# Scaled copies of v in quarters and normalising products in halves on two engines, VectorE's reciprocal for the sums, and another set of ordering numbers in a fused attention and Mish kernel

## The chip, the core and the metric

The kernel runs on one core of a Trainium2 chip. The metric is the device time of one execution in microseconds (us), given as the median of several runs. Besides these, one execution is recorded by the hardware profiler; all rows below come from that one. TensorE multiplies matrices into PSUM, ScalarE evaluates functions (exponential and tanh here), VectorE and GpSimd do elementwise work, SyncE issues most of the DMAs. GpSimd does not read PSUM in this kernel.

## The reference

One input `x` of 2048 tokens by 640 goes through attention with 32 heads of 20 and through a dense layer with Mish; a sigmoid gate per token mixes the two.

```
qkv = (x @ wqkv)                       # 640 -> 3 x 32 heads x 20
scores = einsum("bhqd,bhkd->bhqk", q, k) * Dh ** -0.5
o = einsum("bhqk,bhkd->bhqd", softmax(scores), v)
a = o.reshape(B, S, D) @ wo
h = x @ w1 + b1                        # 640 -> 1536
b = (h * tanh(softplus(h))) @ w2       # Mish, 1536 -> 640
g = sigmoid((x * gate_w).sum(-1))
out = g * a + (1 - g) * b
```

## The kernel before

**Tiling.** Queries go in 4 chunks of 512, heads in 8 groups of 4 (20 rows of a head stand in 32 partitions, so the four heads of a group lie on the four row groups of TensorE). A *unit* is one head's scores for 128 keys by 512 queries: one PSUM bank. There are 2048 units, ordered by (chunk, head group); the last group's queries are cut into two halves of 256.

**A slot.** Three units form a slot; there are 683. `emit_s` puts the three score matmuls (line 1378) into one of two triples of PSUM banks, `emit_e` lets ScalarE take the exponential of the slot in one instruction (line 1400, into the ring `ETS`). In many slots (`choose`) the third unit is given to VectorE instead: ScalarE then takes two units, a *pair*, and `emit_x` evicts the third (line 1450) as a 16-bit integer that, read as a half-precision number, is a first approximation of the exponential. Up to four such units of one head group make a *batch*; `close` adds two shifted versions of the batch (lines 1486 to 1488), and `emit_off` multiplies all three by v on TensorE (line 1720), the third one by a *scaled copy* of v. Scores of slot s+2 need the banks that the exponential and the eviction of slot s have read.

**Scaled copies.** `VW` holds v times 199/256 for the head group in work. `scale` (lines 1674 to 1701) writes it when a group ends: 21 times as one VectorE instruction of 1344 columns, in the first groups as four quarters of 336 columns while v is still being made.

**Sums and normalising.** v has a column of ones, so row 0 of each head's product holds the softmax sums. At a group's end `group_done` copies the accumulated bank to `OUNG` (VectorE, line 1905), moves the four rows of sums through a DMA into `RR`, 128 partitions by 16 (line 1923, queue SP), and `invert` raises them to the power -1 on GpSimd (line 1927). A DMA writes them to `SUMS` in DRAM (line 1930), four more (`spread`, line 1936) read them back into `BCT`, each row repeated over 32 partitions, and `times` (line 1857) multiplies `OUNG` by `BCT`. The product goes to VectorE or, whole (`PARTS = 1`), to GpSimd. Its result is moved by four or five DMAs into the packed layout of the output projection (`move`, line 1850). All these DMAs stand in SyncE's one queue in the order of the program, with the projections' moves (lines 724, 751) and weight loads (lines 997, 1003, 1015).

**The Mish part.** `mish` runs per 1024 columns: tanh on ScalarE (line 1071), then scalars (line 1095) and four products (line 1104) on VectorE; a product may go in quarters to GpSimd.

**What sets the order.** The program is written by a planner (`Plan`, `attention`) that keeps a clock for each engine and adds costs from the table of constants at the top (`EXP`, `WIDE`, `SPREAD_TAIL`, ...). Jobs that are not tied to a slot wait in lists (`norm` for inverting and normalising, `scaled` for the copies, `blend` for Mish, `soon` for shifts); `work` lets VectorE take those that are ready before its next eviction, `settle` offers the head of a list to GpSimd if it fits behind VectorE's last instruction of kind "L" (one that reads and writes SBUF) and before VectorE's clock. `choose` compares VectorE's lead over ScalarE, corrected by `NUDGE[s // 8]`, with thresholds (`BEHIND`, `IDLE`), and decides which slots become pairs. A number in that table so moves rows everywhere behind it. On the chip each engine works its own list strictly in order and waits on semaphores.

## Time and profile before

| | |
|---|---|
| runs (us) | 753.31, 754.74, 753.92; median 753.92 |
| profiled execution (us) | 755.81, of it a span of 754.0 from the first to the last instruction |
| granted TensorE clock, mean | 0.998 |
| exponentials | 683: 492 pairs, 191 triples |
| VectorE evictions of score banks (line 1450) | 492 |
| first and last exponential start (us) | 9.39, 745.1 |

In the rows below PE is TensorE (PEld its weight loads), ACT ScalarE, DVE VectorE, POOL GpSimd, SPq SyncE's DMA queue. A row of the groups gives line, engine, operation, output and inputs with shapes, the count, then busy time in us and the mean duration of one in ns, then the engine's idle time in front of them in us and what ended it. A timeline row gives start and duration in us, and in brackets the idle time of the engine before it with what ended that. A row of the stretches gives the stretch, its length, and busy time and count for PE, PEld, DVE, ACT and POOL, the granted clock, the DMA share and GB/s.

### The profile page before, as it was taken

The numbers are of one execution on the slowest core, as the hardware profiler recorded it, in microseconds if no ns is written. First come the engines' busy times: TensorE is split into PE (matmuls) and PEld (weight loads), VectorE is DVE, ScalarE is ACT, GpSimd is POOL, SyncE is SP. The second block draws the span as 40 slices with busy tenths as digits, with TensorE's granted clock in tenths as the row PEclk, the third lists the DMA queues.
The fourth block names the chain that finished last, engine by engine and source line by source line (L and its number), as shares of the span: only waits on it lengthen the run. The fifth ranks groups of instructions, "written<-read, shape, count | busy, mean of one in ns | idle before, by whom it ended". The sixth has DMA issues, their size and how long they took to land.

```text
span 754.0 us, 19649 instructions
## 1 busy us (share of the span) xinstructions
PE 707.4 (94%) x8065; PEld 266.4 (35%) x8065; DVE 703.4 (93%) x1298; ACT 736.5 (98%) x715; POOL 188.6 (25%) x162
## 2 busy tenths in 40 slices
PE   8999999999998999999999999999999999999996
PEld 4334333333332343233333334333333333323232
DVE  4878898999898999989999999999999999999995
ACT  6999999999999999999999999999999999999996
POOL 8111101333212420212213322213204232223111
PEclk9999999999999999999999999999999999999999
DMA  8321321321233215112113302102222122011001
GB/s 188 105 63 42 99 70 35 101 67 53 65 107 101 70 47 163 39 42 56 54 44 108 95 21 73 60 21 76 82 55 71 55 60 80 20 33 31 18 18 47
DMA packets 81675, 49.62 MB, mean 66 GB/s; under 512 B 25474, under 2 KB 77562, under 8 KB 81578
## 3 DMA queue, kind: packets, MB, share of 16 engines
q1 hardware_dynamic: 80810, 48.16, 22.7%
q8 instruction: 67, 1.10, 0.6%
q14 instruction: 30, 0.25, 0.1%
q10 hardware_dynamic: 656, 0.10, 0.1%
q0 software_dynamic: 112, 0.01, 0.0%
HBM read 36.10 MB, written 7.52 MB: 58 GB/s over the span
## 4 chain that ended last, share of the span: by engine, by line
ACT 86%; PE 7%; DVE 3%; DMA 2%; POOL 0%; issue 0%; SPq 0%
ACT ETS L1400 83%; ACT REG L1071 2%; PE PS L1378 2%; PE PS L1720 2%; PE PS L575 2%; ACT W2R L1071 1%; DVE QT L1450 1%; DMA OTN<-in_A_x_dram 1%; DMA SUMS<-RR 1%; DMA BCT<-SUMS 1%; DVE KT L1450 0%; PE PS L785 0%; POOL RR L1927 0%; DMA RR<-OUNG 0%; PE PS L2152 0%
## 5 line engine op out<-in xcount | busy, mean ns | idle before, releaser
L1400 ACT ACTIVATE ETS<-PS 128x1024 bf16<-128x1024 f32 (+1 forms) x683 | 715.7, 1263 | 5.4 <-PE PS L1378 4.9
L1378 PE MATMUL PS<-QT,KT 32*128 32x512 bf16 (+1 forms) x2112 | 267.3, 378 | 34.0 <-ACT ETS L1400 23.7
L1927 POOL TENSOR_TENSOR RR<-RR,NEG 128x16 f32<-128x16 f32 x31 | 93.9, 3029 | 268.8 <-DMA RR<-OUNG 268.8
L1720 PE MATMUL PS<-ETS,V_all 128*21 128x512 bf16 (+1 forms) x1606 | 156.8, 375 | 0.0
L1378 PEld LDWEIGHTS PS<-QT,KT 32*128 32x128 bf16 x2112 | 67.7, 91 | 250.4 <-ACT ETS L1400 212.1
L1104 POOL TENSOR_TENSOR U<-U 128x256 f16<-128x256 f16 x77 | 50.9, 661 | 215.6 <-DVE U L1095 176.8
L1450 DVE TENSOR_SCALAR QT<-PS 128x512 int16<-128x512 f32 x123 | 82.4, 682 | 2.6 <-PE PS L1378 1.9
L575 PE MATMUL PS<-XB,REG 128*32 128x256 bf16 (+3 forms) x824 | 80.5, 294 | 2.0 <-DVE OUTT L1185 1.5
L1450 DVE TENSOR_SCALAR OTN<-PS 128x512 int16<-128x512 f32 x109 | 73.3, 681 | 2.3 <-PE PS L1378 2.0
L575 PE MATMUL PS<-W2R,HB 128*128 128x320 bf16 (+1 forms) x645 | 72.4, 300 | 0.2
L1450 DVE TENSOR_SCALAR PADS<-PS 128x512 int16<-128x512 f32 x101 | 67.9, 682 | 4.8 <-PE PS L1378 4.6
L575 PEld LDWEIGHTS PS<-XB,REG 128*32 128x32 bf16 (+1 forms) x824 | 39.5, 97 | 32.1 <-issue 21.1
L1720 PEld LDWEIGHTS PS<-ETS,V_all 128*21 128x21 bf16 x1606 | 39.1, 90 | 30.0 <-issue 25.5
L575 PEld LDWEIGHTS PS<-W2R,HB 128*128 128x128 bf16 (+1 forms) x645 | 33.1, 97 | 29.1 <-issue 14.7
L1450 DVE TENSOR_SCALAR KT<-PS 128x512 int16<-128x512 f32 x54 | 36.7, 684 | 4.0 <-PE PS L1378 3.7
L1104 DVE TENSOR_TENSOR U<-U 128x1024 f16<-128x1024 f16 (+3 forms) x71 | 38.6, 544 | 0.0
L1450 DVE TENSOR_SCALAR REG<-PS 128x512 int16<-128x512 f32 x56 | 38.0, 682 | 0.1
L1048 DVE TENSOR_TENSOR HB<-PS,B1T 128x512 bf16<-128x512 f32 x48 | 32.7, 681 | 0.4 <-PE PS L575 0.2
L1095 DVE TENSOR_SCALAR U<-U 128x1024 f16<-128x1024 f16 x72 | 30.1, 418 | 0.5
L1488 DVE TENSOR_SCALAR QT<-QT 128x2048 int16<-128x2048 int16 (+2 forms) x43 | 28.6, 667 | 0.7 <-PE PS L1720 0.7
L1104 POOL TENSOR_TENSOR HB<-U,HB 128x256 bf16<-128x256 f16 x28 | 18.7, 669 | 38.1 <-DVE U L1104 25.6
L1720 PE MATMUL PS<-QT,V_all 128*21 128x512 f16 x280 | 28.2, 388 | 0.0
(176 smaller groups left out, 801.8 us busy)
## 6 DMA issues: line engine op xcount, KB each, us to landing
REG<-in_B_w_dram SPq DMA_DIRECT2D x36, 320.0 KB, 3.2
BCT<-SUMS SPq DMA_DIRECT2D x124, 64.0 KB, 2.0
W2R<-in_B_w_dram SPq DMA_DIRECT2D x12, 320.0 KB, 3.4
KT<-KS SPq DMA_DIRECT2D x28, 128.0 KB
QT<-QS SPq DMA_DIRECT2D x112, 20.0 KB
QS<-WOQ SPq DMA_DIRECT2D x16, 128.0 KB, 1.7
KS<-OTN SPq DMA_DIRECT2D x16, 128.0 KB, 2.6
W2R<-in_B_w_dram SPq DMA_DIRECT2D x1, 1920.0 KB, 8.3
```

What stands on the lines that cost most here:

```text
L575: op = e.matmul(PS[at, bank, cols], w[:, at], x, start=start, stop=stop, **({"tile_position": (0, i * rows)} if parts > 1 else {}))
L1048: ev = dve(lambda e: e.tensor_tensor(hb, PS[:, bank, :].rearrange("p (i t) -> p i t", i=2), bias, ALU.add), [last, b_load, *b_read.get(hc ...
L1071: ex = pl.add("act", lambda e: e.activation(U, h, AF.Tanh, scale=0.5, bias=-MISH_AT), [ev, u_free[0]], cost=0.95)
L1095: return lambda e: e.tensor_scalar(dst, src, *ops)
L1104: return lambda e: e.tensor_tensor(dst[:, at], one[:, at], two[:, at], ALU.mult)
L1378: op = pl.add("pe", lambda e, i=i, g=real(g), tile=tile, j=j, cols=cols, c=c, of_q=of_q: e.matmul(scores(s)[:, i, cols], KT[32 * j:32 * j ...
L1400: e_op[s] = pl.add("act", lambda e: e.activation(EXPS[:, at:at + n, :], scores(s)[:, 0:n, :], AF.Exp, scale=SCALE, bias=LIFT if fast else ...
L1450: ev = dve_by(lambda e: e.tensor_scalar(block(batch["y"], n, I16), scores(s)[:, 2, :], SCALE * ULPS, BIAS, ALU.mult, ALU.add), [s_op[s], * ...
L1488: op = pl.add("dve", lambda e, sp=sp: e.tensor_scalar(some_of(home, sp, I16), some_of(y, sp, I16), by, None, ALU.add), deps, cost=each, ki ...
L1720: lasts[n] = pl.add("pe", lambda e, v=v, j=j, src=src[:, cols], of_q=of_q, count=count: e.matmul(PS[32 * j:32 * j + EW, bank, of_q], v, sr ...
L1927: r = (pl.add("pool", lambda e: e.tensor_tensor(RR[:, :], RR[:, :], NEG[:, :].to_broadcast([P, 16]), ALU.pow), [got, m_neg], cost=INVERT) ...
```

## The change

Four pieces of program and the table of numbers change.

1. `scale` offers the whole copy to GpSimd in quarters of 336 columns: each goes to GpSimd if it fits (`ASIDE_V = 0.6`), what is left goes to VectorE in one instruction. VectorE is held back from it for `AWAIT_V = 2` us of planned time, unless the copy is needed at once (`urgent`). Later copies wait for quarters that GpSimd still writes.
2. `PARTS = 2`: the normalising product goes in halves of 256 columns, and `AWAIT = 3` holds VectorE back from it for 3 us of planned time after the spread sums.
3. `ON_DVE = 1`: `invert` uses VectorE's reciprocal in place of GpSimd's power.
4. A Mish chain's steps wait for the last step of the chain before (`formed`); with GpSimd's quarters this orders the shared buffers.
5. Some thirty constants change, and `NUDGE` has a number for four slots (171 numbers) where it had one for eight (87).

```diff
-STREAM = 0.38
-SPUN = 0.95
+STREAM = 0.46
+SPUN = 0.5
...
-PARTS = 1
+PARTS = 2
 MPARTS = 4
-AWAIT_2 = 0.2
+AWAIT_2 = 0.8
...
+AWAIT_V = 2
+ASIDE_V = 0.6
+RISK_SP = 0.6
+ON_DVE = 1
-LANDED = 1.6
-SEEN = 10
-SPREAD_TAIL = 2.1
+LANDED = 1.8
+SEEN = 8
+SPREAD_TAIL = 1.8
...
-AWAIT = 0
+AWAIT = 3
...
-BEYOND = 0.4
-SOONER = 8
+BEYOND = 0.5
+SOONER = 12
...
-BEHIND = 10.0
+BEHIND = 9.5
...
@@ def settle
-                for todo in (blend, norm):
+                for todo in (scaled, blend, norm):
@@ def patient
-            return now["step"] < NSLOT - CALM_END and pl.now["dve"] < op.t1 + wait
+            return not now.get("urgent") and now["step"] < NSLOT - CALM_END and pl.now["dve"] < op.t1 + wait
@@ def mish
-                        last[0] = pl.add(eng, fn, [last[0], *more], cost=ASIDE_1 if more else cost, kind="L")
+                        last[0] = pl.add(eng, fn, [last[0], *more, *formed], cost=ASIDE_1 if more else cost, kind="L")
...
                 def done(op):
+                    formed[0] = op
@@ def choose
-            late = max(0.0, pl.now["dve"] - pl.now["act"]) - NUDGE[s // 8]
+            late = max(0.0, pl.now["dve"] - pl.now["act"]) - NUDGE[s // 4]
@@ def scale
+            reads = [*scaled_read, *dict.fromkeys(op for op in copies.values() if op.eng == "pool")]
             copies.clear()
-            reads = list(scaled_read)
...
-                scaled.append((cost, run, deps, 0))
+                if n < 4:
+                    scaled.append((cost, run, deps, 0))
+                    return
+                made = []
...
+                def beside(dep):
+                    i = len(made)
+                    copies[i] = pl.add("pool", each(range(i, i + 1)), [*need(), dep], cost=ASIDE_V, kind="L")
+                    made.append(copies[i])
+                    entry[0] = cost * (3 - i) / 4 + 0.06
+                    return i == 3
+
+                def rest():
+                    some = range(len(made), 4)
+                    op = pl.add("dve", each(some), need(), cost=entry[0])
+                    copies.update(dict.fromkeys(some, op))
...
+                entry = [cost, rest, free, 0, None, (lambda: made[-1] if made else deps() or None, ASIDE_V, beside)]
+                scaled.append(entry)
@@ def invert
-                     if fast else pl.add("dve", lambda e: e.reciprocal(RR[:, :], RR[:, :]), [got], cost=0.25))
+                     if fast and not ON_DVE else pl.add("dve", lambda e: e.reciprocal(RR[:, :], RR[:, :]), [got], cost=0.17))
```

In sum over the program: pairs 492 to 493, triples 191 to 190. VectorE gets 31 reciprocals; its whole copies of v go from 21 to 4, with 10 of three quarters, 6 of a half and one quarter more; its normalising products into `OTN` from 27 whole to 14 whole and 8 halves. GpSimd loses the 31 powers and 4 whole products, and gets 25 quarter copies, 26 half products and 10 more quarters of Mish products. Filler matmuls on TensorE (line 2152) go from 51 to 32.

Three places show how rows move. The first is VectorE's list where the twelfth group's product and the next group's copy of its bank (COPY OUNG) stand, about 313 us into the profile. Before:

```order
L1450 TENSOR_SCALAR REG<-PS 128x512
L1857 TENSOR_TENSOR OTN<-OUNG,BCT 128x512
L1905 COPY OUNG<-PS 128x512
L1450 TENSOR_SCALAR QT<-PS 128x512
L1488 TENSOR_SCALAR QT<-QT 128x2x1024
L1488 TENSOR_SCALAR PADS<-PADS 128x2048
L1450 TENSOR_SCALAR QT<-PS 128x512
L1450 TENSOR_SCALAR REG<-PS 128x512
```

The same place in the changed kernel, where line 1895 is the product, 1943 the copy, 1457 an eviction, 1495 a shift, 980, 2080 and 2082 maxima for a guard, and 1967 the reciprocal:

```order
L1895 TENSOR_TENSOR OTN<-OUNG,BCT 128x512
L1943 COPY OUNG<-PS 128x512
L1457 TENSOR_SCALAR QT<-PS 128x512
L1457 TENSOR_SCALAR PADS<-PS 128x512
L980 TENSOR_REDUCE OUTT<-PS 128x1
L2080 TENSOR_REDUCE OUTT<-OUTT 128x4
L2082 TENSOR_TENSOR OUTT<-OUTT 128x1
L1457 TENSOR_SCALAR QT<-PS 128x512
L1495 TENSOR_SCALAR QT<-PADS 128x2x1024
L1967 RECIPROCAL RR<-RR 128x16
L1457 TENSOR_SCALAR QT<-PS 128x512
```

The product stands right ahead of the copy in both; behind the copy, seven instructions later, VectorE now has the reciprocal, which waits for the DMA of the sums, and evictions behind it.

The second is SyncE's queue at the same place, where `OTN<-OTN` are the moves of the finished product and `RR<-OUNG` is the DMA of the sums. Before:

```order
L2045 DMA OUTT<-OUTT 1x80x1
L2045 DMA XS<-OUTT 1x80x1
L2045 DMA GROW<-OUTT 1x128x1
L1850 DMA OTN<-OTN 20x512 x4
L1923 DMA RR<-OUNG 128x1x16
L724 DMA QS<-WOQ 128x512
L1930 DMA SUMS<-RR 128x16
```

In the changed kernel:

```order
L1974 DMA BCT<-SUMS 32x512 x4
L1888 DMA OTN<-OTN 20x512 x4
L1961 DMA RR<-OUNG 128x1x16
L2083 DMA OUTT<-OUTT 1x80x1
L2083 DMA XS<-OUTT 1x80x1
L2083 DMA GROW<-OUTT 1x128x1
L1968 DMA SUMS<-RR 128x16
```

The four moves stand ahead of the sums' DMA in both; the guard's three DMAs have moved behind it.

The third is GpSimd's list from its first normalising work on. Before:

```order
L1927 TENSOR_TENSOR RR<-RR,NEG 128x16 x4
L1857 TENSOR_TENSOR OTN<-OUNG,BCT 128x512
L1927 TENSOR_TENSOR RR<-RR,NEG 128x16
L1104 TENSOR_TENSOR U<-U 128x256 x7
L1104 TENSOR_TENSOR HB<-U,HB 128x256 x3
L1927 TENSOR_TENSOR RR<-RR,NEG 128x16
```

In the changed kernel, where line 1713 is a quarter of the scaled copy:

```order
L1895 TENSOR_TENSOR OTN<-OUNG,BCT 128x256 x8
L1111 TENSOR_TENSOR U<-U 128x256 x4
L1713 TENSOR_SCALAR VW<-V_all 128x336
L1111 TENSOR_TENSOR U<-U 128x256 x2
L1111 TENSOR_TENSOR HB<-U,HB 128x256
L1895 TENSOR_TENSOR OTN<-OUNG,BCT 128x256
```

The powers are gone; half products and quarter copies stand between the quarters of the Mish products.

## The prediction

> **What bounds the kernel.** I read the head of the page first, then the chain that ended last, then the stretches.

> ```profile
> span 754.0 us, 19649 instructions
> PE 707.4 (94%) x8065; PEld 266.4 (35%) x8065; DVE 703.4 (93%) x1298; ACT 736.5 (98%) x715; POOL 188.6 (25%) x162
> ACT 86%; PE 7%; DVE 3%; DMA 2%; POOL 0%; issue 0%; SPq 0%
> L1400 ACT ACTIVATE ETS<-PS 128x1024 bf16<-128x1024 f32 (+1 forms) x683 | 715.7, 1263 | 5.4 <-PE PS L1378 4.9
> ```

> ScalarE works 736.5 of 754.0 us, 715.7 of them on the 683 exponentials, and the chain runs through it for 86% of the span. A term counts only if it shortens ScalarE's list or the times in which it waits. Its length per exponential comes from two stretches that hold one shape each:

> ```profile
> L1400 ACT ACTIVATE ETS<-PS 128x1024 bf16<-128x1024 f32 x11 | 10.3, 1152 | 0.0
> L1400 ACT ACTIVATE ETS<-PS 128x1536 bf16<-128x1536 f32 x8 | 11.1, 1700 | 0.0
> ```

> Neighbours overlap, so a step is the busy time less one duration, over the number less one: (10.3 - 1.15)/10 = 0.92 us for two blocks, (11.1 - 1.70)/7 = 1.34 us for three. The block left out of a pair goes to VectorE. The page before has 492 pairs and 191 triples: 492 x 0.92 + 191 x 1.34 = 709 us, so about 7 of the 715.7 us are starts that came late without an idle row, beside 4.9 us of idle time that the page puts on TensorE's scores. These twelve us are all that an order can win between the first exponential and the last.

> VectorE is the engine that could be in the way, most of all in the second half:

> ```profile
> 400.00:500.00 100.00, 93.57 (x1101) 36.83 (x1101) 99.11 (x183) 99.79 (x97) 27.17 (x26) 1.00 0.22 63
> 500.00:600.00 100.00, 94.33 (x1126) 37.29 (x1123) 99.52 (x193) 100.00 (x97) 26.72 (x24) 1.00 0.22 61
> ```

> The third and fourth busy times are VectorE's and ScalarE's: 99 and 100 of 100 us. What stands still on VectorE reaches ScalarE nearly whole, as the largest wait of the run shows:

> ```profile
> 238.94 0.69 DVE L1857 TENSOR_TENSOR OTN<-OUNG,BCT 128x512 bf16<-128x512 f32 x1 [1.89 <-DMA BCT<-SUMS]
> 239.55 0.68 DVE L1450 TENSOR_SCALAR PADS<-PS 128x512 int16<-128x512 f32 x1
> 240.15 0.42 DVE L1095 TENSOR_SCALAR U<-U 128x1024 f16<-128x1024 f16 x1
> 240.48 0.68 DVE L1450 TENSOR_SCALAR PADS<-PS 128x512 int16<-128x512 f32 x1
> 240.81 1.45 ACT L1400 ACTIVATE ETS<-PS 128x1536 bf16<-128x1536 f32 x1 [1.54 <-PE PS L1378]
> ```

> VectorE waited 1.89 us for the spread sums, the eviction behind the product came late, TensorE could not refill the bank, and ScalarE idled 1.54 us: 0.8 us for each us. The same rows give VectorE's steps: an eviction lasts 0.68 but the next starts after 0.60, a 1024-wide half-precision scalar lasts 0.42 and steps 0.33; a step is 0.08 less than the duration.

> **Part 1, the exponentials.** By the two orders there are 493 pairs and 190 triples now: one triple turned into a pair, 0.92 - 1.34 = **-0.4 us** on ScalarE. The 24 tanh calls stay, and head and tail of the order are alike within an instruction or two.

> **Part 2, the inversion moves to VectorE.** Rows for one ordinary place, and for the prices:

> ```profile
> 684.51 0.68 DVE L1905 COPY OUNG<-PS 128x512 f32<-128x512 f32 x1
> 685.22 0.63 SPq L1923 DMA_DIRECT2D RR<-OUNG  x1
> 687.20 3.08 POOL L1927 TENSOR_TENSOR RR<-RR,NEG 128x16 f32<-128x16 f32 x1 [2.30 <-DMA RR<-OUNG]
> L1927 POOL TENSOR_TENSOR RR<-RR,NEG 128x16 f32<-128x16 f32 x31 | 93.9, 3029 | 268.8 <-DMA RR<-OUNG 268.8
> L940 DVE RECIPROCAL GATE<-OMG 128x16 f32<-128x16 f32 x1 | 0.3, 253 | 0.0
> ```

> The power took GpSimd 3.03 us and VectorE nothing; a reciprocal of the same shape takes VectorE 0.25 us, a step of 0.17: 31 x 0.17 = +5.3 us of VectorE. The chain of a group gets 2.8 us shorter, which helps nobody as long as the product is not waited for. The new thing is a **wait**: the sums land 687.20 - 684.51 = 2.69 us after the copy started, and before, GpSimd waited for that (268.8 us, at no cost). Now VectorE reaches the reciprocal after as much work as the order puts between, and all its evictions queue behind it. Adding up the steps (0.60 for a shift of a whole batch too) I get between copy and reciprocal 2.65 to 8.05 us, median 3.8. Against 2.69 us no place but two is tight. Late landings are what counts, and the queue makes them:

> ```profile
> 312.92 0.68 DVE L1857 TENSOR_TENSOR OTN<-OUNG,BCT 128x512 bf16<-128x512 f32 x1
> 314.33 3.12 SPq L1850 DMA_DIRECT2D OTN<-OTN  x4
> 317.50 0.60 SPq L1923 DMA_DIRECT2D RR<-OUNG  x1
> 319.45 3.43 POOL L1927 TENSOR_TENSOR RR<-RR,NEG 128x16 f32<-128x16 f32 x1 [13.46 <-DMA RR<-OUNG]
> ```

> Four moves of a finished group take SyncE 3.12 us, and the sums' DMA stands behind them. In the changed order the same product stands again right ahead of the copy (shown under the change). From its start: 0.7 until the moves may go, 3.17, then 1.95 to land, 5.8 us; VectorE is at the reciprocal after 0.6 + 3.8 = 4.4 us and waits **1.4 us**. At the copies that I count as 8th and 17th (31 in all), the same sum gives 0.7 and 0.4. Together 2.5 us of VectorE, by 0.8 **+2.0 us** on ScalarE. The bounds are 0 (work between stretches) and the case in which each late landing of before comes back at its group. The worst of them:

> ```profile
> 294.72 0.42 SPq L1003 DMA_DIRECT2D W2R<-in_B_w_dram  x1
> 295.19 0.79 SPq L1923 DMA_DIRECT2D RR<-OUNG  x1
> 303.09 2.89 POOL L1927 TENSOR_TENSOR RR<-RR,NEG 128x16 f32<-128x16 f32 x1 [26.94 <-DMA RR<-OUNG]
> ```

> Behind the big weight load the sums took 7.9 us. There the new order has 8.05 us between, the most of all. Nine of the 31 landed 0.5 us late or more; set against the new distances they would cost 11.3 us of VectorE, **+9.1 us** on ScalarE.

> **Part 3, the product in halves, and waited for longer.** The old wait of 1.89 us goes if the spread sums are there: **-1.5 us** (0 if not). The soonest a product went was

> ```profile
> 115.28 0.35 SPq L1930 DMA_DIRECT2D SUMS<-RR  x1
> 120.60 1.27 POOL L1857 TENSOR_TENSOR OTN<-OUNG,BCT 128x512 bf16<-128x512 f32 x1 [5.35 <-DMA BCT<-SUMS]
> ```

> 5.3 us after the sums' return; between reciprocal and VectorE's share of the product the new order has 5.8 us of work at least, 9 mostly.

> **Part 4, VectorE's load.**

> ```profile
> L1691 DVE TENSOR_SCALAR VW<-V_all 128x1344 bf16<-128x1344 bf16 x21 | 11.7, 559 | 0.0
> L1691 DVE TENSOR_SCALAR VW<-V_all 128x336 bf16<-128x336 bf16 x12 | 2.8, 242 | 0.2
> L1857 DVE TENSOR_TENSOR OTN<-OUNG,BCT 128x512 bf16<-128x512 f32 x27 | 18.4, 681 | 1.9 <-DMA BCT<-SUMS 1.9
> L1104 DVE TENSOR_TENSOR U<-U 128x1024 f16<-128x1024 f16 x26 | 17.7, 680 | 0.0
> L1104 POOL TENSOR_TENSOR U<-U 128x256 f16<-128x256 f16 x77 | 50.9, 661 | 215.6 <-DVE U L1095 176.8
> ```

> Of the 21 whole copies 4 stay, 10 shrink to three quarters and 6 to a half: in steps (0.42 whole, 0.16 for a quarter, 0.33 and 0.25 between) 8.8 becomes 6.5, -2.3, and the 1.3 us go by which the 21 lay above 0.50 each. Products: 27 whole become 14 and 8 halves, 16.2 to 11.1, -5.1. GpSimd takes 115 quarters of activation products where it took 105: -1.5. With +5.3 for reciprocals VectorE loses 4.9 us of work. As both engines are full side by side over hundreds of us, I count half of it on ScalarE: **-2.5 us**, the middle between 0 (ScalarE alone sets the pace) and -4.9 (VectorE does).

> GpSimd gives up 93.9 us and gets 25 copies, 26 half products and 10 quarters. A quarter copy stands in no row; the nearest is

> ```profile
> L675 POOL COPY REG<-REG 128x400 bf16<-128x400 bf16 x1 | 0.5, 519 | 1.3 <-DMA REG<-in_A_wqkv_dram 1.3
> 447.96 1.49 POOL L1104 TENSOR_TENSOR U<-U 128x256 f16<-128x256 f16 x2 [7.22 <-DVE U L1095]
> 449.00 0.82 DVE L1691 TENSOR_SCALAR VW<-V_all 128x1344 bf16<-128x1344 bf16 x1
> 477.56 0.49 DVE L1691 TENSOR_SCALAR VW<-V_all 128x1344 bf16<-128x1344 bf16 x1
> ```

> so about 0.45 us, at most the 0.66 of a two-input piece: each fits beside an eviction of 0.68. The lower rows show the danger: a whole copy beside a GpSimd product took 0.82 us, one alone 0.49. The new pieces are placed behind VectorE's last SBUF instruction, beside evictions. I take 0 for collisions; bounds -1.0 (the removed ones) and +1.6 on ScalarE (51 pieces, a fifth colliding as 4 of 21 copies did, 0.33 each, half passed on). [...]

> **Part 5, the order itself.** The numbers that set it alter the place of nearly every row. Filler matmuls fall from 51 to 32, the rest of TensorE's work is the same. I give this no term; its size is bounded by the twelve us above, either way by a few. One of the old losses was not the order's:

> ```profile
> 314.00:317.50 3.50, 3.50 (x30) 0.85 (x28) 2.74 (x5) 2.45 (x3) 0.00 (x0) 0.51 0.10 17
> 317.05 1.02 ACT L1400 ACTIVATE ETS<-PS 128x1024 bf16<-128x1024 f32 x1 [1.05 <-PE PS L1378]
> ```

> The granted clock was 0.51 there and ScalarE lost 1.05 us idle; it may or may not come again.

> **Sum.** The profiled execution took 755.81 us, 1.8 beside its span, and 1.9 more than the median of 753.92. -0.4 + 2.0 - 1.5 - 2.5 = -2.4, so 753.4 for a profiled run, **751.5 us** against the median.

> **Rivals.** (A) *The reciprocal holds VectorE up.* For it: no work separates late landings from evictions any more, and 1.89 us of such waiting cost 1.54 before. Against: most places have over a us to spare. With every late landing back it gives 751.5 - 2.0 + 9.1 = 758.6; it decides (over 755.4) once such waits cost ScalarE 5.9 us. Chance 0.16. (B) *ScalarE paces alone.* The saved VectorE work was hidden anyway, the new wait takes the old one's place: -0.4 + 2.0 - 1.5 + 0 = +0.1, 754.0. For it: ScalarE 100.00 in 500 to 600, where it lost next to nothing. Chance 0.27. (C) *All relief reaches ScalarE and no landing is late*: -0.4 - 1.5 - 4.9, 747.1. Chance 0.10. (D) The collisions of part 4 at +1.6 alone end within B's bounds and are counted there.

> **Numbers.** The forecast has 0.47, with its own range 749.0 to 752.4. Runs of this kernel differ so that 0.2%, 1.5 us, is about what a measurement tells from no change. Forecast and C are faster, 0.57; B is the same, 0.27; A is slower, 0.16. The range 748.0 to 756.0 leaves out most of C and most of A, 0.18.

> **What would show it.** Part 2: idle rows of VectorE before the reciprocal, named after the DMA of the sums, some 2.5 us in few places, the largest behind the four moves; over 7 us would be A. Part 3: no idle row before the product. Part 4: VectorE's busy time near 698, GpSimd's near 125, quarter copies under 0.66 us; a longer one would reach past the eviction and stretch VectorE's shifts. Rival B shows as a shorter VectorE with ScalarE's idle time unchanged near 5 us. What I can be most wrong in is part 5: a stretch in which the new order overfills TensorE shows as ScalarE idle behind scores with VectorE waiting too.

## The result, and the profile after

The changed kernel takes **761.67 us** (median of 5 runs, 759.34 to 763.41) against 754.06 us for the kernel before in the same session: a ratio of 1.0083, 95% interval 1.0059 to 1.0107. It is slower; the forecast was 751.5 us, and its range ended at 756.0. The profiled execution took 760.77 us with a span of 758.8, which is 4.8 more than the span before. Of these, 1.4 us came before the end of the last exponential (747.81 us against 746.41) and 3.4 behind it; but the profiled execution before had lost time itself (1.9 us above its median, with a stretch of half clock at 314 us), so the shares are taken from the experiments' medians. Lines are those of the changed kernel from here on: scores 1385, exponentials 1407, evictions 1457, product 1895, copy of the sums' bank 1943, their DMA 1961, reciprocal 1967. From the page after, the head, the chain, the exponentials and GpSimd's quarters of the scaled copy:

```profile
span 758.8 us, 19700 instructions
PE 709.5 (94%) x8051; PEld 265.3 (35%) x8051; DVE 701.9 (93%) x1328; ACT 736.8 (97%) x716; POOL 144.0 (19%) x189
ACT 80%; PE 11%; DVE 3%; DMA 3%; SPq 1%; issue 0%; ACTq 0%; DVEq 0%
L1407 ACT ACTIVATE ETS<-PS 128x1024 bf16<-128x1024 f32 (+1 forms) x683 | 716.2, 1264 | 6.6 <-PE PS L1385 6.3
L1713 POOL TENSOR_SCALAR VW<-V_all 128x336 bf16<-128x336 bf16 x25 | 28.7, 1155 | 94.3 <-PE PS L1758 49.4
```

ScalarE works as long as before (736.8 us against 736.5) in a longer span; its part of the chain fell from 86% to 80%, TensorE's rose from 7% to 11%. So ScalarE got no more work; it is held up more often, and less of the end runs through it. VectorE's waits for DMAs, from the view that groups waits (total us, times, longest):

```profile
DVE RR L1967 <- DMA RR<-OUNG: 3.5, 2, 1.8
DVE OTN L1895 <- DMA BCT<-SUMS: 0.4, 1, 0.4
```

The wait for the product shrank from 1.9 to 0.4 us, and 3.5 us of waits for the sums came in two places. One is at the thirteenth copy, as forecast (1.64 us, forecast 1.4). The other, at the fourth, was not forecast; from the timeline:

```profile
105.54 0.69 DVE L1943 COPY OUNG<-PS 128x512 f32<-128x512 f32 x1
106.28 3.85 SPq L1888 DMA_DIRECT2D OTN<-OTN  x5
110.17 0.48 SPq L730 DMA_DIRECT2D KS<-OTN  x1
110.70 0.62 SPq L1961 DMA_DIRECT2D RR<-OUNG  x1
112.64 0.25 DVE L1967 RECIPROCAL RR<-RR 128x16 f32<-128x16 f32 x1 [1.84 <-DMA RR<-OUNG]
113.58 0.40 PE L1385 MATMUL PS<-QT,KT 32*128 32x512 bf16 x3 [1.05 <-DVE KT L1457]
114.01 1.02 ACT L1407 ACTIVATE ETS<-PS 128x1024 bf16<-128x1024 f32 x1 [0.77 <-PE PS L1385]
...
320.94 0.25 DVE L1967 RECIPROCAL RR<-RR 128x16 f32<-128x16 f32 x1 [1.64 <-DMA RR<-OUNG]
```

Five moves and one more DMA of SyncE stand ahead of the sums' DMA, which starts 5.2 us after the copy. VectorE waits 1.84 us, TensorE 1.05 for the eviction behind the reciprocal, ScalarE 0.77 for the scores. The kernel before had a late landing at this group too, which cost nothing there because GpSimd waited for it:

```profile
106.30 0.68 DVE L1905 COPY OUNG<-PS 128x512 f32<-128x512 f32 x1
112.36 2.90 POOL L1927 TENSOR_TENSOR RR<-RR,NEG 128x16 f32<-128x16 f32 x1 [23.04 <-DMA RR<-OUNG]
```

The sums were there 6.1 us after the copy's start, and 7.1 in the changed kernel (112.64 against 105.54). But the loss did not end there. The stretches of the changed kernel (PE is the first busy time after the length, the granted clock the third number from the end):

```profile
112.80:116.22 3.42, 1.96 (x23) 0.83 (x23) 3.42 (x8) 2.08 (x3) 0.00 (x0) 1.00 0.22 59
116.22:119.63 3.41, 3.41 (x27) 1.41 (x24) 2.37 (x4) 2.71 (x3) 0.00 (x0) 0.50 0.22 62
747.68:751.10 3.42, 1.70 (x38) 0.65 (x31) 2.53 (x6) 0.18 (x2) 0.00 (x0) 1.00 0.11 29
751.10:754.51 3.41, 2.89 (x17) 1.19 (x9) 1.02 (x2) 0.89 (x2) 1.68 (x2) 0.50 0.26 79
```

Twice TensorE was busy for under 2.0 of 3.41 us, and in the 3.41 us behind it its clock was 0.50: 27 matmuls fill 116.22 to 119.63 without a gap, and ScalarE works 2.71 of 3.41 us. The second pair of rows is the end of the program, where the timeline shows:

```profile
748.40 0.45 DVE L1926 STREAM_TRANSPOSE U<-PS 128x256 f32<-128x256 f32 x1
749.95 0.54 DVE L1192 SCALAR_TENSOR_TENSOR HB<-PS,GATE,W2R 128x320 bf16<-128x320 f32 x1
750.54 0.77 PE L581 MATMUL PS<-WOQ,QT 128*32 128x320 bf16 x16 [1.62 <-DVE HB L1192]
751.64 2.34 PE L581 MATMUL PS<-WOQ,QT 128*128 128x320 bf16 x8
753.49 1.68 DVE L2315 SCALAR_TENSOR_TENSOR HB<-PS,GATE,W2R 128x640 bf16<-128x640 f32 x2 [3.00 <-PE PS L581]
```

Three projection tasks are left behind the last products with v, where the kernel before had one. One of them is evicted behind the last group's transposes (749.95), TensorE waits 1.62 us for that eviction, and the last eight matmuls then take 2.34 us at half clock. From the start of the last group's product (749.61) to the last evictions it takes 3.88 us; before it took 0.97:

```profile
748.33 0.42 DVE L1894 TENSOR_TENSOR QT<-PS,U 128x256 bf16<-128x256 f32 x1
...
749.30 1.68 DVE L2277 SCALAR_TENSOR_TENSOR HB<-PS,GATE,W2R 128x640 bf16<-128x640 f32 x2 [0.54 <-PE PS L575]
```

### The profile page after: what moved, and what is told of

It is laid out like the page before. It is cut to its first block, busy times and chain, and to the rows that moved or that the text cites. A ratio compares the mean times of both kernels' runs of the same rounds, so it can differ in the third digit from the quotient of the medians.

```text
span 758.8 us, 19700 instructions
## 1 busy us (share of the span) xinstructions
PE 709.5 (94%) x8051; PEld 265.3 (35%) x8051; DVE 701.9 (93%) x1328; ACT 736.8 (97%) x716; POOL 144.0 (19%) x189
## 4 chain that ended last, share of the span: by engine, by line
ACT 80%; PE 11%; DVE 3%; DMA 3%; SPq 1%; issue 0%; ACTq 0%; DVEq 0%
ACT ETS L1407 77%; PE PS L1758 3%; PE PS L1385 3%; PE PS L581 2%; ACT REG L1077 2%; DMA QS<-WOQ 2%; PE PS L920 1%; PE PS L2190 1%; ACT W2R L1077 1%; SPq L757 1%; DMA RR<-OUNG 1%; DMA OTN<-in_A_x_dram 1%; DVE QT L1457 0%; DVE KT L1457 0%; DVE V_all L930 0%
## 5 line engine op out<-in xcount | busy, mean ns | idle before, releaser
L1111 POOL TENSOR_TENSOR U<-U 128x256 f16<-128x256 f16 x92 | 60.3, 656 | 228.9 <-DVE U L1102 149.4
L1457 DVE TENSOR_SCALAR OTN<-PS 128x512 int16<-128x512 f32 x120 | 81.5, 685 | 1.2 <-PE PS L1385 0.8
L581 PE MATMUL PS<-W2R,HB 128*32 128x320 bf16 (+1 forms) x687 | 72.0, 300 | 0.8 <-DVE OUNG L1943 0.5
L1895 POOL TENSOR_TENSOR OTN<-OUNG,BCT 128x256 bf16<-128x256 f32 x24 | 17.4, 727 | 217.6 <-issue 87.4
L1457 DVE TENSOR_SCALAR PADS<-PS 128x512 int16<-128x512 f32 x69 | 46.9, 687 | 3.9 <-PE PS L1385 3.7
L1713 POOL TENSOR_SCALAR VW<-V_all 128x336 bf16<-128x336 bf16 x25 | 28.7, 1155 | 94.3 <-PE PS L1758 49.4
L581 PEld LDWEIGHTS PS<-W2R,HB 128*32 128x32 bf16 (+1 forms) x687 | 33.6, 97 | 28.6 <-issue 13.6
L1111 DVE TENSOR_TENSOR U<-U 128x768 f16<-128x768 f16 (+3 forms) x71 | 36.8, 519 | 0.1
L1495 DVE TENSOR_SCALAR OTN<-OTN 128x2048 int16<-128x2048 int16 (+2 forms) x52 | 29.0, 571 | 0.3 <-PE PS L1758 0.3
L1495 DVE TENSOR_SCALAR QT<-QT 128x2048 int16<-128x2048 int16 (+1 forms) x41 | 28.2, 691 | 0.1
## 6 DMA issues: line engine op xcount, KB each, us to landing
W2R<-in_B_w_dram SPq DMA_DIRECT2D x1, 1920.0 KB, 10.9
```

Of the source, the lines that this page charges most:

```text
L581: op = e.matmul(PS[at, bank, cols], w[:, at], x, start=start, stop=stop, **({"tile_position": (0, i * rows)} if parts > 1 else {}))
L1111: return lambda e: e.tensor_tensor(dst[:, at], one[:, at], two[:, at], ALU.mult)
L1457: ev = dve_by(lambda e: e.tensor_scalar(block(batch["y"], n, I16), scores(s)[:, 2, :], SCALE * ULPS, BIAS, ALU.mult, ALU.add), [s_op[s], * ...
L1495: op = pl.add("dve", lambda e, sp=sp: e.tensor_scalar(some_of(home, sp, I16), some_of(y, sp, I16), by, None, ALU.add), deps, cost=each, ki ...
L1713: return lambda e: e.tensor_scalar(VW[:, rows, :], V_all[:, rows, g * HG:(g + 1) * HG, :].rearrange("p t h e -> p t (h e)"), SCALED, None, ...
L1895: op = pl.add(eng, lambda e: e.tensor_tensor(to[:, cols], src[:, cols], BC[:, cols], ALU.mult), [*deps, *reads()], cost=WIDE * share + 0.0 ...
```

## The experiments

Three theories were tested: that VectorE's waits before the reciprocal and the end of the program make the loss; that VectorE's load as such reaches ScalarE; that the new order as a whole, or GpSimd's new pieces, are worse. So that the order stays what the planner wrote, the edits act on the finished lists. `put_off` takes an instruction, with those that follow from it, out of the program and puts it behind the n-th next VectorE instruction:

```python
def put_off(first, others, n):
    ops = fast.ops
    at = ops.index(first)
    for op in others:
        ops.remove(op)
    ops.remove(first)
    while n:
        ...
        n -= ops[at].eng == "dve"
        at += 1
    ops[at:at] = [first, *others]
```

The kernel before had medians of 756.1 to 756.7 us beside these kernels, so ratios to it are what is compared; 0.001 is 0.76 us. Three dots in an edit stand for lines left out.

**1. The end.**

```diff
-            bank = (filler[0], 5, 4)[now["spot"] % 3]
+            bank = (5, 4, filler[0])[now["spot"] % 3]
```

> Changed kernel, its order kept up to the last scores; only the banks of the three projection tasks behind them are taken in the order 5, 4, 7 and no longer 7, 5, 4. Theory (the end costs 3.3 us because TensorE waits for the eviction that stands behind the last group's transposes, and then runs at half clock): the stretch from the end of the last exponential to the end of the span falls from 10.9 us to 7.6 to 8.3, the idle row of 1.6 us before the 16 projection matmuls and the clock window at 751 to 754 go, the time falls by 2.5 to 3.5 us to about 758.5. Rival (the last group's chain of transposes, product, last matmuls and evictions sets the end whatever the banks): the stretch stays over 10 us, the time falls by less than 1 us.

Ratio 1.0054 (1.0033 to 1.0075), 761.09 us. The idle row and the half clock at 751 us went, and the last evictions end 4.5 us behind the last exponential where it was 7.4. The whole stretch from the last exponential to the end of the span fell only from 11.0 to 9.5 us, short of what was expected, because the last output landed 5.0 us behind them where it was 3.6. This run's clock still fell at 116 us after a longer wait of VectorE (2.9 us), so the median doesn't decide it. Experiment 3 shows the end by its rows.

**2. The two reciprocals later.**

```diff
+    for n, k in ((3, 4), (12, 4)):
+        put_off(inverted[n][0], [inverted[n][1]], k)
```

> Changed kernel; the reciprocals of the 4th and the 13th group and the return of their sums stand four VectorE instructions later, everything else stays in its place. Theory (VectorE's wait at those two places lets TensorE idle, and the half clock that follows doubles the loss): idle time of VectorE before the reciprocals falls from 3.5 us to under 0.5, the clock window at 116 to 120 goes with the same number of filler matmuls, ScalarE's late starts at 114 to 121 and 320 to 324 go, the time falls by 3 to 4.5 us to about 758. Rival 1 (the fewer filler matmuls of the new order, not the wait, let the clock fall): the window at 116 to 120 stays and the time falls by 1 to 2 us. Rival 2 (ScalarE loses the same time somewhere behind, since VectorE is full anyway): within 1 us of the changed kernel's 761.7.

Ratio **1.0004** (0.9987 to 1.0021), 757.31 us, more won than the 3 to 4.5 us expected. The timeline at the fourth group:

```profile
111.45 0.62 SPq L1961 DMA_DIRECT2D RR<-OUNG  x1
113.39 0.25 DVE L1967 RECIPROCAL RR<-RR 128x16 f32<-128x16 f32 x1
```

The sums' DMA starts no earlier than in the changed kernel, and nobody waits: VectorE does evictions and shifts meanwhile. No window of half clock lies at 116 us any more, with the same 32 filler matmuls, so rival 1 falls; the time gained rules out rival 2. This execution still has a window of half clock in its middle, from 315.89 to 319.31 us, where the kernel before had one too; so the edit took away the one at 116 us and not all of them.

**3. Both.**

> Both edits in one kernel. If the two losses are apart, the time falls by their sum, 5.5 to 8 us, to 753.7 to 756.2, about the time before. If something else is behind the slower time, it stays over 758.

Ratio **0.9988** (0.9971 to 1.0005), 755.86 us: level with the kernel before. Rows of the end without the bank edit (late_inverse), from the projections behind the last product to the last evictions:

```profile
747.25 0.42 DVE L1932 TENSOR_TENSOR QT<-PS,U 128x256 bf16<-128x256 f32 x1
...
748.19 0.73 PE L581 MATMUL PS<-WOQ,QT 128*32 128x320 bf16 x16 [1.63 <-DVE HB L1192]
...
750.09 1.68 DVE L2316 SCALAR_TENSOR_TENSOR HB<-PS,GATE,W2R 128x640 bf16<-128x640 f32 x2 [1.96 <-PE PS L581]
```

and with it (tail_and_inverse):

```profile
746.91 0.42 DVE L1932 TENSOR_TENSOR QT<-PS,U 128x256 bf16<-128x256 f32 x1
...
747.94 1.68 DVE L2316 SCALAR_TENSOR_TENSOR HB<-PS,GATE,W2R 128x640 bf16<-128x640 f32 x2 [0.15 <-PE PS L581]
```

From product to last evictions 2.84 us became 1.03: the end cost 1.8 us, and 1.1 more where the half clock met it (at 751.64 in the changed kernel eight matmuls took 2.34 us, here 1.25). The medians differ by 0.0016, 1.2 us, with intervals that overlap, so the time alone doesn't show it.

**4. Only the reciprocal, in the order of before.**

```diff
+    for op in inverted:
+        op.eng = op.key = "dve"
+        op.fn = lambda e: e.reciprocal(RR[:, :], RR[:, :])
+        op.deps = op.deps[:1]
```

> Kernel before with its order as it was; only the 31 powers of GpSimd become reciprocals of VectorE at their place in the list, products and copies stay whole. From the trace of before, VectorE would come too early in four places, by 1.71 (4th group), 0.35, 0.52 and 0.39 us, 3.0 us in all, and gets 31 x 0.17 = 5.3 us more work. Theory (only waits that let TensorE idle count, and the first of them brings a half clock): VectorE idle 2.5 to 3.5 us before the reciprocal, a clock window within 6 us behind the 4th group's, the time rises by 1.5 to 4 us to about 757. Rival 1 (VectorE's work passes to ScalarE at 0.8): (3.0 + 5.3) x 0.8 = 6.6 us more, 760.7. Rival 2 (neither passes on): within 1 us of 754.1.

Ratio 1.0053 (1.0033 to 1.0073), 760.31 us, 4.0 us up; VectorE waited 4.3 us before reciprocals in four places, the largest again the fourth group's:

```profile
113.02 0.25 DVE L2372 RECIPROCAL RR<-RR 128x16 f32<-128x16 f32 x1 [2.28 <-DMA RR<-OUNG]
...
114.53 0.39 PE L1378 MATMUL PS<-QT,KT 32*128 32x512 bf16 x3 [1.90 <-DVE KT L1450]
...
114.96 2.37 ACT L1400 ACTIVATE ETS<-PS 128x1024 bf16<-128x1024 f32 x2 [1.63 <-PE PS L1378]
```

The expected window of half clock didn't come in this execution, though TensorE idled 1.90 us.

**5. Its waits moved away, and a miss.**

```diff
+    for n, k in ((1, 1), (3, 5), (8, 2), (12, 2), (13, 2)):
+        put_off(inverted[n][0], [inverted[n][1]], k)
```

> The kernel of before_inverse_dve; in the five groups whose sums landed at or behind VectorE's arrival (2nd, 4th, 9th, 13th, 14th) the reciprocal and the return of the sums stand 1, 5, 2, 2 and 2 VectorE instructions later. VectorE keeps the 5.3 us of reciprocals but should wait under 0.6 us before them (4.3 us then). Theory (the waits make the loss): the time falls from 1.0053 of before to 1.000 to 1.0015. Rival (the work itself passes on by half or more): 1.0035 or more.

Ratio 1.0059 (1.0039 to 1.0079), 760.49 us: nothing was won. No wait stood before a reciprocal any more; the rows at the ninth group tell where it went:

```profile
241.22 0.69 DVE L1857 TENSOR_TENSOR OTN<-OUNG,BCT 128x512 bf16<-128x512 f32 x1 [3.84 <-DMA BCT<-SUMS]
...
243.31 1.45 ACT L1400 ACTIVATE ETS<-PS 128x1536 bf16<-128x1536 f32 x1 [3.70 <-PE PS L1378]
```

That product had waited 1.89 us already in the kernel before. With the reciprocal later, the sums return later, and it waits 3.84; ScalarE idles 3.70, and the clock is at half from 241.20 to 248.03 us. VectorE stands at both ends of that chain of DMAs. So a further kernel moved both ends:

```diff
+    put_off(products[8][0], products[8][1:], 4)
+    put_off(products[11][0], [*products[11][1:], *copied[12]], 1)
+    for n, k in ((1, 1), (3, 5), (12, 2), (13, 2)):
+        put_off(inverted[n][0], [inverted[n][1]], k)
```

> Kernel before with reciprocals on VectorE, as in before_inverse_dve, and with the places in which VectorE waited cleared on both sides: the reciprocals of the 2nd, 4th, 13th and 14th group later by 1, 5, 2 and 2 VectorE instructions, the 9th left where it was, and the products of the 9th and 12th group (the latter with the copy behind it) later by 4 and 1. Theory (in before_inverse_later the wait went from the 9th reciprocal to the 9th product, which stood idle 3.8 us; work alone costs nothing): VectorE idle before reciprocals and products under 2 us in all (6.4 in before_inverse_dve), ratio 0.998 to 1.001. Rival (5.3 us of reciprocals pass on by half or more whatever waits there are): 1.0035 or more.

Ratio **0.9992** (0.9976 to 1.0008), 756.00 us. VectorE waits 1.6 us before reciprocals and 0.7 before products, a little over the 2 us expected and 4.1 less than the 6.4 of before_inverse_dve; the time fell by 0.0061, 4.6 us. Part of that is the old wait of the ninth product, which experiment 6 takes alone. Against that kernel (0.9955) 2.8 us (1.9 either way) are left for 2.3 us of waits and 5.3 us of reciprocals together, so the work itself passes on less than its length, and how much less stays open.

**6. The product alone, in the order of before.**

```diff
+    put_off(products[8][0], products[8][1:], 4)
```

> Kernel before; only the product of the 9th group (238.94 us, VectorE idle 1.89 us in front) and its four moves stand four VectorE instructions later. Theory (a wait of VectorE costs ScalarE four fifths of itself, and can be had back by work put in front of it): the idle row before the product and ScalarE's late start of 1.9 us at 240.8 go, the time falls by 1.2 to 2.2 us, ratio 0.997 to 0.9985. Rival (ScalarE loses it again within the next microseconds, or the later moves are missed): ratio 0.999 to 1.001.

Ratio **0.9955** (0.9937 to 0.9974), 753.50 us, faster than both kernels and by more than expected. The row at the place, and the stretch in which the kernel before had lost its clock:

```profile
239.38 0.68 DVE L1857 TENSOR_TENSOR OTN<-OUNG,BCT 128x512 bf16<-128x512 f32 x1
```

```profile
309.99:313.40 3.41, 2.19 (x29) 0.73 (x33) 3.27 (x8) 3.41 (x5) 0.00 (x0) 1.00 0.05 7
313.40:316.81 3.41, 3.06 (x39) 0.81 (x28) 3.41 (x7) 3.41 (x4) 0.00 (x0) 1.00 0.09 18
```

The wait is gone, and the window of half clock at 314 us as well, 75 us from the edit. That the edit took it away isn't shown: hold_long (experiment 11) is the same program up to 402 us, and its execution was at half clock from 312.95 to 316.36, behind a window in which TensorE was busy for 1.96 us where it is 2.19 here. The mean clock of five of its seven runs was 0.999 or 1.000; the kernel before beside it lay between 0.995 and 0.999.

**7. VectorE's load, taken and given.** In the order of before, the second half of 25 products goes to GpSimd:

```diff
+        if fast.ops and op.eng == "dve" and n not in (11, 12):
+            other = Op("pool", lambda e, part=part: part(e, 1), list(op.deps), None)
+            op.fn = lambda e, part=part: part(e, 0)
...
```

> Kernel before with its order as it was; of 25 products that VectorE made whole, the second half goes to GpSimd, nothing else changes. VectorE loses 25 x 0.34 = 8.5 us, GpSimd gets 25 x 0.73 = 18 us. Theory (the relief of VectorE is hidden behind ScalarE): within 1 us of before, ratio 0.9985 to 1.0015, VectorE's busy time 694 to 696 and its idle time grown by as much. Rival 1 (half passes on): -4.2 us, 0.9944. Rival 2 (the two engines hinder each other, so the halves cost more than they save): over 1.002, with VectorE's other instructions stretched beside the pieces.

Ratio 0.9992 (0.9979 to 1.0005), 0.6 us less. But the relief itself didn't come as counted. From its page the busy times, and from the groups the halves of the product:

```profile
PE 700.7 (93%) x8027; PEld 266.5 (35%) x8065; DVE 702.4 (93%) x1298; ACT 736.4 (98%) x715; POOL 210.0 (28%) x187
...
L1863 DVE TENSOR_TENSOR OTN<-OUNG,BCT 128x256 bf16<-128x256 f32 x25 | 11.8, 471 | 1.7 <-DMA BCT<-SUMS 1.6
L1863 POOL TENSOR_TENSOR OTN<-OUNG,BCT 128x256 bf16<-128x256 f32 x25 | 20.4, 816 | 72.1 <-DMA BCT<-SUMS 72.1
```

VectorE's products fell by 5.2 us (18.4 to 13.2, with two left whole), yet its busy time only by 1.0, from 703.4 to 702.4, where 694 to 696 was expected: side by side with GpSimd's halves its own took 0.471 us (0.413 in tail_and_inverse, where halves lie beside evictions) and the 218 shifts 2.1 us more in all. The first half of rival 2 is seen, its effect on the time not. As a test of what relief is worth this run is weak.

Then the other direction, from tail_and_inverse, with GpSimd's pieces back on VectorE, for each instruction of VectorE that had given some away:

```diff
...
+            op.fn = fn
+            for other in made:
+                fast.ops.remove(other)
...
```

> The kernel of tail_and_inverse, with work of GpSimd back on VectorE in its place: all 25 quarter copies (VectorE's share is a whole copy again) and 8 of the half products (9 groups keep both halves on GpSimd). VectorE gets 25 x 0.16 + 8 x 0.34 = 6.7 us more. Theory (ScalarE sets the pace and VectorE's load reaches it only through single waits): the time stays within 1 us of tail_and_inverse, a ratio of 0.998 to 1.000 to before. Rival 1 (half of VectorE's load passes on, as the prediction took it): +3.4 us, about 1.003. Rival 2 (all of it): +6.7 us, about 1.008.

Ratio 0.9987 (0.9972 to 1.0001) against 0.9988 without. VectorE's busy time grew by 2.8 us (702.1 to 704.9), not by 6.7, since a copy of three quarters takes nearly as long as a whole one (0.44 against 0.53). These 2.8 us cost nothing; the two intervals together leave some 1.7 us to either side, which excludes that all of it passes on, and doesn't decide about half. That GpSimd makes 25 quarter copies shows no cost in the time either.

**8. The power back on GpSimd, in the new order.**

```diff
...
+        op.eng = op.key = "pool"
+        op.fn = lambda e: e.tensor_tensor(RR[:, :], RR[:, :], NEG[:, :].to_broadcast([P, 16]), ALU.pow)
...
```

> Changed kernel, its order kept; the 31 reciprocals of VectorE are GpSimd's powers again, at the same places of the order. Theory (the change loses by VectorE's waits for the sums, and by the end): no idle row of VectorE before an inversion, GpSimd 94 us more busy, the products not waited for much more (their sums come 2.8 us later; bound +2 us where VectorE is at the product early), the time falls by 3 to 6 us, ratio 1.000 to 1.005; the 3 us at the end stay. Rival 1 (the new order of the rest makes the loss): ratio stays over 1.006. Rival 2 (the powers hold up GpSimd's quarter copies and halves, so that TensorE waits for these): ratio over 1.006 with idle rows of TensorE named after VW or of VectorE after GpSimd.

Ratio 1.0134 (1.0107 to 1.0161), 768.05 us, slower still, against the 1.000 to 1.005 of the theory. Rival 2 came true, on the Mish pieces and the halves:

```profile
525.75 2.89 POOL L2410 TENSOR_TENSOR RR<-RR,NEG 128x16 f32<-128x16 f32 x1 [2.68 <-DMA RR<-OUNG]
528.60 0.61 POOL L1111 TENSOR_TENSOR U<-U 128x256 f16<-128x256 f16 x1
529.25 0.56 DVE L1111 TENSOR_TENSOR U<-U 128x768 f16<-128x768 f16 x1 [2.13 <-POOL U L1111]
530.56 0.39 PE L1385 MATMUL PS<-QT,KT 32*128 32x512 bf16 x3 [1.78 <-DVE REG L1457]
```

A Mish piece stands behind the power, and VectorE waits for the piece; by the waits' view 12.3 us in nine places. This order counts on a GpSimd that never stands for a DMA.

**9. The thirteenth group, a second miss.** From tail_and_inverse, product and copy behind two evictions, and the reciprocal one instruction later:

```diff
+    put_off(products[11][0], [*products[11][1:], *copied[12]], 2)
+    for n, k in ((3, 4), (12, 5)):
+        put_off(inverted[n][0], [inverted[n][1]], k)
```

> The kernel of tail_and_inverse; further, the product of the 12th group with its four moves, and the 13th group's copy with its sums' DMA behind it, stand two VectorE instructions later, so that two evictions go first, and the 13th reciprocal one more behind. Theory (product and copy ahead of the evictions let TensorE idle 1.2 us at 313 and a half clock follows): the idle row of TensorE there falls under 0.5, ScalarE's late starts at 314 to 319 fall from 2.1 to under 0.8, the clock window at 315 to 318 goes in most runs, the time falls by 1 to 2 us to a ratio of 0.996 to 0.9975. Rival (the eight wide-tile matmuls and the scores' order there make the loss): within 0.5 us of tail_and_inverse, 0.9988.

Ratio 0.9990 (0.9975 to 1.0006): no gain. TensorE's idle row of 1.19 us there fell to 0.53, but the clock was half from 315.3 to 318.7 all the same and ScalarE idled 1.41 us at 317.44. That is as the rival has it; which of its two reasons counts wasn't tested.

**10. The changed kernel once more.**

> The changed kernel once more, unaltered, beside the other three and on their chip, since the gains of the mended versions are differences against it. From its first runs: ratio 1.006 to 1.011 to before; VectorE idle 3 to 5 us before the reciprocals in two places, mean clock of its runs 0.991 to 0.997.

Ratio 1.0068 (1.0045 to 1.0090), 761.83 us; VectorE idle 3.9 us before two reciprocals, mean clocks of 0.990 to 0.996.

**11. Holds of VectorE.** What one standstill costs was measured by itself, in before_product_later, whose clock is nearly whole:

```diff
+    for n in [673, 743, 817, 888, 968, 1043, 1116, 1191]:
+        fast.ops.insert(fast.ops.index(mine[n]), Op("dve", lambda e: e.tensor_reduce(
+            GROW[:, 0:1], flat[:, 0:1856], AX.X, ALU.max), [], None))
```

> The kernel of before_product_later with eight extra instructions on VectorE, between 400 and 690 us some 40 us apart, each a maximum over 1856 numbers of a finished block of v into a tile that is no longer used, about 2 us long: VectorE stands still for evictions as it does in a wait. Theory 1 (idle of TensorE lets the clock fall): TensorE idles 1 to 2 us behind each hold, at least three of the eight are followed within 8 us by a window of 3.4 us at half clock, the mean clock falls from 0.999 to 0.991 to 0.996, and the time rises by 8 x 1.6 us and 1 to 1.5 us for each window, some 16 to 20 us. Theory 2 (the clock goes its own way): no more windows than before, mean clock 0.998 or more, the time rises by 8 x 1.6 = 13 us.

> The same with holds over 640 numbers, about 0.7 us. Theory (single short pieces of VectorE's work are hidden, long standing still is not): the time rises by 0 to 2 us, that is by under a third of the eight holds' 5.6 us. Rival (four fifths of any standing still reach ScalarE): +4.5 us. No clock windows by either.

Long holds (2.07 us each): ratio 1.0178 (1.0156 to 1.0200), over 0.9955 that is 2.24% or 16.9 us (2.2 either way) for 8 x 1.99 = 15.9 us of standstill. Part of it is the clock, 0.992 in the median run against 0.999 in before_product_later. Over the 219 runs of the experiments, each set against the mean of its kernel, 0.001 of mean clock goes with 0.5 us; by that estimate the clock has 3.5 of the 16.9 us, and the standstill itself passes on 13.4 of 15.9, or 0.84. Short holds (0.81 us): 1.0017 (1.0000 to 1.0033), 0.6% or 4.7 us (1.9 either way) for 5.8 us, nearer the rival than the theory; in the profiled executions the spans differ by 2.9 us. Stretches behind three of the long holds:

```profile
442.72:446.13 3.41, 1.62 (x26) 0.54 (x27) 3.41 (x5) 1.95 (x3) 0.00 (x0) 0.99 0.10 30
446.13:449.54 3.41, 3.41 (x24) 1.11 (x16) 2.48 (x5) 2.36 (x2) 0.00 (x0) 0.51 0.04 11
527.98:531.39 3.41, 1.56 (x13) 0.53 (x13) 3.38 (x7) 2.51 (x4) 1.24 (x2) 1.00 0.03 2
531.39:534.80 3.41, 3.25 (x40) 1.59 (x40) 2.44 (x6) 1.61 (x2) 0.98 (x2) 0.50 0.22 67
572.44:575.85 3.41, 2.17 (x18) 1.14 (x18) 3.38 (x8) 2.10 (x3) 0.67 (x1) 1.00 0.00 0
575.85:579.26 3.41, 2.46 (x39) 0.92 (x37) 3.38 (x7) 3.41 (x4) 1.35 (x2) 1.00 0.35 98
```

Two of the eight holds were followed by a window of half clock, those that left TensorE busy for 1.62 and 1.56 us of 3.41; one that left it 2.17 was not. Its runs had mean clocks of 0.990 to 0.995, those of hold_short 0.996 to 1.000. A third window of half clock in the middle stands ahead of the first hold (312.95, the first hold at 402.5). Two lies between the two theories' counts (three or more, none); the last section sets such windows against the share of them that matmuls filled.

## Why the prediction was wrong

Two steps failed, and one loss was left out. **Part 2** mis-sized the wait and left out the half clock behind it: +2.0 us forecast, 4.8 to 6.0 measured. **Part 4** let half of the work that VectorE loses reach ScalarE, -2.5 us: none of it showed. The end of the program, which part 1 took as alike, cost some 1.2 us by the medians and 1.8 by the rows. Point by point:

- *What bounds the kernel*: held up to the last exponential. ScalarE's busy time stayed, and its idle time behind scores rose from 4.9 to 6.3 us. Behind the last exponential, where 3.4 of the 4.8 us of span arose, other engines and the output's DMAs set the time.
- *Part 1, -0.4 us*: the exponentials changed as counted. But "head and tail of the order are alike within an instruction or two" was wrong: three projection tasks stand at the end where one stood, one of them evicted behind the transposes. That is +1.8 us by the rows, 1.2 by medians whose intervals overlap, and up to 1.1 more at half clock.
- *Part 2, +2.0 us*: the mechanism and one place were right. At the thirteenth copy 1.4 us were forecast and 1.64 measured, in part by luck: the sums landed 6.5 us after the product's start where 5.8 was counted, and VectorE was at the reciprocal after 4.9 where 4.4 was. Of the other two places forecast nothing came. The fourth group was missed: it was set against the ordinary 2.69 us from copy to landing, though the rows before show 6.1 there; such late landings entered only the upper bound. VectorE idled 3.5 to 4.5 us in three executions where 2.5 was forecast, and taking that away won 4.8 to 6.0 us (1.0068 and 1.0083 against 1.0004, about 2 us either way). The factor of 0.8 itself was near (0.84 by the long holds). What the sum lacked beside the fourth group is the half clock: the median run has a mean clock of 0.994 or 0.995 in the changed kernel and 0.997 in late_inverse, by the estimate of experiment 11 some 1 to 1.5 us.
- *Part 3, -1.5 us*: the product's wait went (1.9 to 0.4 us). Alone it is worth 3.4 us in the order of before (0.9955, 1.4 us either way), at least the wait itself.
- *Part 4, -2.5 us*: didn't show. With the two waits and the end mended, what is left of the change is -0.9 us (0.9988; -2.2 to +0.4), where parts 1, 3 and 4 together promised -4.4; the kernel before with one wait mended has 0.9955. Nor was VectorE relieved as counted: its busy time fell by 1.5 us and not by 4.9. Products (-5.2), Mish pieces (-1.4) and reciprocals (+5.2) came as counted, with time in which two neighbours overlap counted once as in the busy time; the copies lost 2.2 where 3.6 was counted, and the rest of its list grew by 2.1 with the new order. And 2.8 us given back cost nothing. "Side by side over hundreds of us" is no evidence that relief of one engine frees the other. How much of a small piece passes on the runs bound only roughly. The quarter copy took 1.155 us where 0.45 was taken, GpSimd 144.0 us where 125 was; neither showed in the time. Collisions at 0 held nearly, with GpSimd's pieces mostly beside evictions: VectorE's evictions took 0.685 us against 0.682 before, its shifts of a whole batch 0.689 against 0.684, its half products 0.414 where side by side with GpSimd's they took 0.471 (experiment 7).
- *Part 5, no term*: in the middle that was fair, since with the two waits and the end mended the new order is level with the old one (0.9988). The end is counted above. The half clock at 314 us, which this part set apart from the order, stood behind a window in which TensorE was busy for 1.95 of 3.41 us (rows in the last section); that it had nothing to do with the order was not shown. The twelve us that were to bound this part bound what an order can win, not what it can lose.

The forecast was -2.4 us against the kernel before, measured were +5.1 to +6.3 (1.0068, 1.0083). Of the 7.5 to 8.7 us between, part 2 has 2.8 to 4.0, parts 1, 3 and 4 together 3.5, and the end 1.2. Each is a difference of medians and good to some 2 us.

Of the rivals, A named the mechanism and its side, and its 758.6 us came nearest. Its number is in part luck: it holds 9.1 us for late landings, where 4.8 to 6.0 came from two places, and the -2.5 of part 4, which didn't come. B's first half (the saved work was hidden anyway) is at least not contradicted.

## What to carry to other kernels

When an operation that waits for a DMA is moved to the engine whose list is full of evictions, price each place by all that stands ahead of that DMA in its queue, and look at both ends of the chain: putting the first instruction later can hand the wait to the last one. A standstill of 2 us on such an engine passed on some four fifths of its length here (13.4 of 15.9 us in hold_long, the estimate of experiment 11), and with the half clock behind some of them it came to the whole (16.9 us). Eight pieces of 0.8 us passed on most of theirs too (4.7 of 5.8 us in hold_short), while 2.8 us of load given back in small pieces could not be seen in the time: so count no gain for relief before a run shows it. Look up each place's own late landing in the rows before, and compare the last instructions of the two orders row by row; no work behind them hides a wait (the end cost 1.8 us by the rows here).

## What the runs showed of the hardware

```profile
238.93:242.34 3.41, 1.96 (x20) 0.55 (x20) 3.40 (x7) 1.87 (x3) 0.61 (x1) 1.00 0.18 42
310.61:314.02 3.41, 1.95 (x24) 0.50 (x20) 3.27 (x8) 3.41 (x4) 0.00 (x0) 1.00 0.02 1
314.02:317.44 3.42, 3.42 (x30) 0.81 (x28) 2.66 (x5) 2.37 (x3) 0.00 (x0) 0.50 0.10 16
```

At 0.57 busy it went either way. The same idle time of TensorE can so stand before a half window or not, as the edges fall: the place at 313 us left TensorE busy for 1.96 us of a window in hold_long, which half clock followed, and for 2.19 in before_product_later, the same program there, which it didn't follow. One such window takes 0.0023 off the mean clock (half of 3.41 us in 754), by the estimate of experiment 11 some 1.2 us. A window that is gone far from an edit, as in experiment 6, may so be chance. In the changed kernel matmuls still filled 1.96 and 1.70 of 3.41 us of the windows ahead of those two, with longest gaps of 1.05 and 1.62 us. What goes with the half clock beside the share that matmuls fill stays open, and with it the half clock at 315 us in three_places, which followed a window that was 0.70 busy.
